# A recurrent attention kernel followed by a two-layer network: transposing DMAs, two more issuing queues and a new order

## The chip, the cores and the metric

The kernel runs on one core of a Trainium2 chip. The metric is device time in microseconds of one execution; lower is better. The core has five engines with a queue of instructions each: TensorE (PE), VectorE (DVE), ScalarE (ACT), GpSimd (POOL) and SyncE (SP). DMAs are issued from the queues of SP, ACT or POOL and run on 16 shared DMA engines.

## The reference

First a recurrence over 768 steps, for 4 batches and 8 heads of 48 channels:

```
state = zeros(B, H, D, D)
for t in range(S):
    cur = outer(u * k[t], v[t])
    y[t] = r[t] @ (state + cur)
    state = w[t][:, None] * state + outer(k[t], v[t])
```

Then, with y of all heads laid side by side (3072 rows of 384 columns), a hidden layer and an output layer:

```
h = x @ w_in                                  # 384 -> 1024
e = exp(h - max(h)); sm = e / sum(e)
solu = h * sm
ln = (solu - mean(solu)) / sqrt(var(solu) + 1e-6) * g_ln
out = ln @ w_out                              # 1024 -> 384
```

## The kernel before, in words

The rows are cut into 24 units of 128 steps: unit i is chunk i // 4 of batch i % 4. Each unit goes through a chain of stages, and each stage is a small function that issues the instructions of one unit:

- Loads: w, k, r, v of the unit (`LW`, `LK`, `LR`, `LV`; 192 KB each, in runs of 48 floats), into rings of 7 buffers (`NIO`).
- Attention: `lw` takes the log of w on ACT, `cum` sums it along the steps by two matmuls, `ex` takes exponentials, `kp` scales k and r with them on DVE (one tile `kp` of 128 x 2 x 8 x 64, bf16). `krk` and `krr` turn the scaled k and r by four TensorE transposes each into a PSUM tile `kr_ps`, and `kr` copies it to SBUF (tile `kr`, 128 x 8 x 128) on ACT or DVE. `M` multiplies them to scores, `m` copies the scores to SBUF (with the mask on DVE, or on ACT and then `sel` masks on POOL). `p`, `q`, `dg`, `dv` work out the term with u on POOL and DVE, `vb` casts v. `Y` forms y in PSUM, `y` copies it. `S`, `et`, `st` carry the state to the next chunk of the same batch.
- Network: `X` turns y by three TensorE transposes into `x_ps`, `xT` copies that to SBUF, `H` is the hidden layer (24 matmuls), `e`, `he`, `hq` its exponential, product and square, `Oa` and `Ob` the two halves of the output layer with the sums for the normalisation, `sq`, `qm`, `lv` the scale, `o` the scaled output and `out` the store.
- Once: loads of u, g and the two weight matrices (`LU`, `LG`, `LI`, `LO`), constants, casts and centring of the weights (`wi`, `gs`, `gc`, `gw`, `mn`, `mc`, `ce`), u spread over the partitions by a matmul (`us`, `uc`), and `hot`, matmuls on a zero tile.

The order is written out by hand in the string `ORDER`: one word a stage and unit, as `kr4.d`. The letter behind the dot chooses the engine or queue (a ACT, d DVE, p POOL, s SP) or, for TensorE stages, the PSUM slot. The class `InOrder` makes every engine's instructions follow in this order, so an instruction that waits holds back all that stand behind it on its engine. In the kernel before, loads stand on SP and a few on ACT, and all stores on SP. DMAs of SP and ACT share eight semaphores in turn, and a DMA waits before its issue until the one eight places earlier in the order has landed. Scores and state matmuls both read results of `kp`; the first read of a turned k and r is `M`, that of a turned y is `H`. Two functions, `turned_kr` and `turned_x` (`KD`, `XD`), stand in the table of stages and are not used:

```
sp.dma_start_transpose(out=kr_s[i % NKP], in_=kp_t[i % NKP].rearrange("t j h d -> t (j h d)"))
sp.dma_start_transpose(out=xT_t[i % NWK], in_=y_t[i % NWK])
```

The helper at line 89 records nearly all instructions, so rows of the profile are told apart by the names of tiles.

Of the kernel before, what the change touches and what calls it, by code (L numbers as in the profile page):

```python
# [8 lines left out]
F32 = mybir.dt.float32  # L9
# [12 lines left out]
LW0.a LK0.s LU0.a LR0.s LW1.a LW2.s hot4.s3 LG0.s LK1.s lw0 LV0.a cum0.b0 LR1.s us0.s0 ex0 hot2.s3 uc0 lw1 LV1.s  # L22
p0 kp0 LW3.a LK2.a LR2.s krk0.s3 q0 krr0 cum1.b1 kr0.a hot2.s2 LV2.s LK3.a M0.b0 LR3.s p1 gs0.s1 ex1 m0.d
hot3.s3 LI1.s lw2 q1 dg0 cum2.b0 lw3 hot2.s3 kp1 vb0.p LI0.a S0.s2 dv0 vb1.a dg1 hot1.s3 ex2 Y0.is0 et0 LV3.a
cum3.b1 LI2.s p2 kp2 krk1.s3 gc0 LO0.s ex3 st0 LW4.s krk2.s1 q2 krr1 LO1.s krr2 kp3 kr1.a hot3.s2 dv1 LK4.s
kr2.d y0.a p3 M1.b0 LK5.a S1.s2 dg2 krk3.s3 vb2.a m1.d krr3 et1 wi0.a S2.s0 wi1.p M2.b1 st1 X0.s1 kr3.a m2.d
Y1.is2 LR4.s wi2.p et2 y1.a M3.b0 xT0.d LV4.a X1.s3 q3 m3.d H0.b1 dv2 gw1.a dg3 gw2.d e0 Y2.is2 LW5.s xT1.d
gw3.p st2 H1.b0 y2.a he0 lw4 gw0.a X2.s1 LR5.s e1 gw7.d cum4.b1 gw4.d hot2.s3 gw6.d gw5.d ex4 he1 vb3.p mn0.s3
LW6.s LV5.a dv3 xT2.a LK6.s kp4 S3.s0 mc0 Y3.is2 LR6.s lw5 ce6.d krk4.s1 ce3.d hq0.a cum5.b0 ce4.d krr4 ce2.d
H2.b1 ce7.d ex5 LW7.s ce1.d ce5.d ce0.d y3.a LK7.s p4 kp5 et3 Oa0.s3 lw6 e2 LR7.s kr4.d p5 krk5.s2 cum6.b0 st3  # L30
hq1.a Ob0 vb4.p he2 LW8.s q4 krr5 ex6 S4.s1 LK8.s kr5.d sq0 M4.b1 lw7 Oa1.s0 kp6 et4 m4.a LR8.s X3.s2 qm0 st4
vb5.p M5.b0 xT3.a cum7.b1 dg4 sel4 lv0 krk6.s1 LV6.s Ob1 m5.d ex7 LW9.s dv4 lw8 S5.s2 kp7 o0.a krr6 LK9.s p6
cum8.b0 sq1 et5 Y4.ns3 kr6.d ex8 H3.b1 q5 LV7.s y4.d hq2.a kp8 q6 LR9.s krk7.s1 e3 X4.s3 st5 LW10.s vb6.p M6.b0
krr7 xT4.d Oa2.s2 dg5 m6.a LK10.s qm1 kr7.d dv5 krk8.s3 lv1 Ob2 he3 out0 sel6 o1.a lw9 M7.b0 out1 dg6 S6.s1 sq2
m7.a LV8.s hq3.d krr8 cum9.b1 LR10.s Y5.ns0 vb7.p qm2 kr8.d lv2 H4.b0 p7 LW11.s et6 y5.d ex9 st6 p8 lw10 kp9
LV9.s X5.s3 S7.s0 e4 Oa3.s1 q7 o2.d vb8.a he4 out2 cum10.b1 dv6 xT5.a krk9.s2 et7 LK11.s ex10 Y6.ns3 q8 krr9 st7
LV10.s H5.b0 hq4.a kp10 sel7 LR11.s kr9.a y6.d M8.b1 dg7 LW12.s S8.s0 lw11 m8.d Ob3 dv7 et8 e5 LV11.s vb9.p
krk10.s3 st8 X6.s2 LK12.s p9 M9.b1 he5 xT6.a Y7.ns0 sq3 m9.a krr10 LR12.s S9.s2 dg8 cum11.b0 et9 LW13.s y7.d
H6.b1 lw12 dv8 ex11 kr10.d LK13.s p10 qm3 lv3 kp11 Oa4.s0 LR13.s e6 q9 st9 X7.s3 cum12.b0 LW14.s xT7.a Ob4 he6
p11 ex12 LV12.s krk11.s2 sel9 sq4 Y8.ns3 o3.a kp12 H7.b1 hq5.a out3 vb10.p qm4 y8.d q10 LK14.s lv4 dg9 M10.b0 e7  # L40
Oa5.s1 LR14.s m10.d vb11.p q11 o4.a krr11 LW15.s X8.s3 lw13 dg10 Ob5 p12 xT8.a out4 he7 kr11.a S10.s0 dv9 S11.s3
LV13.s dg11 sq5 hq6.a Y9.ns2 vb12.p qm5 cum13.b0 y9.d dv10 LK15.s H8.b1 et10 ex13 st10 LR15.s et11 lw14 kp13
Oa6.s2 LW16.s e8 hq7.d krk12.s0 lw15 M11.b0 p13 st11 LK16.s Ob6 lv5 he8 o5.a q12 krr12 m11.a Y10.ns3 out5 kr12.d
krk13.s1 cum14.b1 LR16.s y10.d sq6 krr13 sel11 ex14 cum15.b0 LW17.s kr13.d Oa7.s0 ex15 qm6 LV14.s kp14 p14
Y11.ns3 lw16 X9.s1 Ob7 kp15 lv6 dv11 LK17.s vb13.a xT9.d p15 o6.a M12.b1 y11.d M13.b0 m12.a X10.s1 out6 m13.d
krk14.s2 q13 S12.s3 LR17.s hq8.a krr14 H9.b1 dg12 LV15.s vb14.p xT10.d sq7 q14 et12 qm7 st12 LW18.s lv7 krk15.s1
dg13 e9 X11.s3 sel12 H10.b0 o7.d kr14.a out7 he9 dv12 LK18.s Y12.ns0 xT11.a p16 krr15 LR18.s Oa8.s2 e10 y12.d
kr15.d q15 LV16.s cum16.b1 he10 S13.s0 ex16 dv13 Ob8 LV17.s et13 kp16 q16 X12.s3 LW19.s Y13.ns1 sq8 xT12.a st13
M14.b0 vb15.p M15.b1 LK19.s m14.a y13.d krk16.s3 S14.s0 hq9.d krr16 LR19.s m15.a S15.s1 p17 qm8 kr16.d H11.b0
LW20.s et14 dg14 lv8 sel14 st14 et15 LK20.s dg15 H12.b1 e11 vb16.p o8.d sel15 st15 out8 lw17 Oa9.s3 he11 LV18.s  # L50
e12 vb17.p dv14 S16.s0 LV19.s hq10.a he12 Ob9 dv15 LR20.s et16 cum17.b0 st16 q17 Y14.ns2 LV20.s ex17 X13.s1
y14.d M16.b1 sq9 Oa10.s0 lw18 kp17 LW21.s m16.a Y15.ns2 qm9 xT13.d LK21.s cum18.b0 hq11.d lv9 krk17.s1 lw19
H13.b1 LR21.s o9.d p18 vb18.a dg16 ex18 LV21.s y15.d dv16 krr17 e13 Ob10 kp18 LW22.s sel16 X14.s3 hq12.a kr17.d
S17.s2 LK22.s cum19.b0 q18 he13 Oa11.s1 xT14.a LR22.s ex19 p19 X15.s3 lw20 M17.b1 out9 xT15.d Ob11 sq10 kp19
vb20.p m17.a LW23.s q19 Y16.ns3 qm10 dg17 et17 vb19.a cum20.b0 p20 LV22.s y16.d lv10 H14.b1 dg18 sq11 ex20 sel17
LK23.s st17 lw21 o10.d LR23.s Oa12.s3 e14 kp20 dv17 krk18.s2 Ob12 out10 hq13.a p21 qm11 he14 krk19.s0 LV23.s
lv11 krr18 q20 cum21.b0 sq12 o11.d krr19 ex21 H15.b1 p22 qm12 kr18.d out11 lv12 kr19.d vb21.p Oa13.s1 dv18 kp21
e15 X16.s2 o12.d Y17.ns0 xT16.a M18.b0 hq14.a y17.d out12 krk20.s3 Ob13 he15 lw22 X17.s0 m18.a krk21.s2 xT17.d
krr20 cum22.b1 dg19 krr21 sq13 sel18 ex22 qm13 S18.s0 dg20 H16.b0 kr20.d hq15.a q21 kr21.d lv13 kp22 Oa14.s3
dv19 e16 dv20 M19.b1 et18 Y18.ns2 he16 m19.a Ob14 lw23 sel19 y18.d M20.b1 sq14 M21.b0 o13.d Oa15.s2 m21.a st18  # L60
out13 m20.d krk22.s1 X18.s0 cum23.b0 xT18.a krr22 Ob15 ex23 hq16.d vb22.p dg21 kr22.a Y19.ns0 q22 kp23 H17.b1
vb23.a dv21 qm14 sq15 y19.d lv14 Y20.ns1 e17 p23 o14.d H18.b0 dg22 out14 sel21 qm15 y20.d lv15 krk23.s0 he17 e18
Oa16.s3 dv22 krr23 o15.a he18 q23 Ob16 kr23.a out15 X19.s1 M22.b1 xT19.d M23.b0 hq17.d X20.s2 S19.s0 xT20.a
hq18.d Oa17.s1 m22.a dg23 Y21.ns2 et19 m23.a sel22 st19 H19.b1 sq16 sel23 qm16 y21.d lv16 Oa18.s0 e19 dv23
X21.s2 Ob17 he19 H20.b0 sq17 o16.d xT21.d out16 Y22.ns3 qm17 e20 Y23.ns2 y22.d Ob18 y23.d hq19.a he20 H21.b1
lv17 o17.d X22.s3 Oa19.s2 e21 out17 xT22.d hq20.d X23.s1 sq18 H22.b0 he21 xT23.d Ob19 qm18 hq21.d e22 H23.b1
sq19 lv18 qm19 he22 Oa20.s3 e23 o18.d hq22.d Oa21.s1 out18 lv19 he23 Ob20 o19.d Ob21 sq20 hq23.d out19 Oa22.s0
sq21 qm20 qm21 lv20 Oa23.s2 lv21 o20.d o21.d out20 Ob22 out21 Ob23 sq22 qm22 lv22 sq23 qm23 o22.d lv23 out22
o23.a out23
# [27 lines left out]
def kernel(  # L97
# [14 lines left out]
    C = 128  # L112
# [20 lines left out]
    def bank(shape, dtype, slot, name):  # L133
# [15 lines left out]
    dve.memset(warm, 0.0)  # L149
    uti_neg = consts.tile([C, C], BF16)  # L150
    pool.memset(uti_neg, -1.0)
    pool.affine_select(out=uti_neg, in_=uti_neg, compare_op=ALU.is_ge, fill=0.0, base=0,
                       pattern=[[1, C]], channel_multiplier=-1)
    uts = consts.tile([C, C], BF16)
    pool.memset(uts, 1.0)
    pool.affine_select(out=uts, in_=uts, compare_op=ALU.is_gt, fill=0.0, base=0,
                       pattern=[[1, C]], channel_multiplier=-1)
    ident_f = consts.tile([C, C], F32)
    pool.memset(ident_f, 0.0)
    pool.affine_select(out=ident_f, in_=ident_f, compare_op=ALU.not_equal, fill=1.0, base=0,  # L160
                       pattern=[[-1, C]], channel_multiplier=1)
    ident = consts.tile([C, C], BF16)
    pool.tensor_copy(out=ident, in_=ident_f)

    halves = consts.tile([C, C], BF16)
    pool.memset(halves, 0.0)
    pool.memset(halves[0:2, :], 1.0)
    pool.affine_select(out=halves[0:2, :], in_=halves[0:2, :], compare_op=ALU.is_ge, fill=0.0, base=0,
                       pattern=[[1, C]], channel_multiplier=-64)
    pool.affine_select(out=halves[0:2, :], in_=halves[0:2, :], compare_op=ALU.is_gt, fill=0.0, base=64,  # L170
                       pattern=[[-1, C]], channel_multiplier=64)
    off_blocks = consts.tile([C, HP, 2], BF16)
    pool.memset(off_blocks, 0.0)
    pool.memset(off_blocks[0:2], -30000.0)
    pool.affine_select(out=off_blocks[0:2], in_=off_blocks[0:2], compare_op=ALU.not_equal, fill=0.0, base=0,
                       pattern=[[0, HP], [-1, 2]], channel_multiplier=1)

    one_col = consts.tile([C, 2], BF16)
    dve.memset(one_col, 1.0)
    inv_col = consts.tile([C, 1], BF16)  # L180
    dve.memset(inv_col, 1.0 / RDF)
    ones_row = consts.tile([1, C], F32)
    dve.memset(ones_row, 1.0)

    lw_t = ring("lw", NLW, [C, H, 64], BF16)
    kp_t = ring("kp", NKP, [C, 2, H, 64], BF16)
    for j in range(max(NLW, NKP)):
        if j < NLW:
            dve.memset(lw_t[j][:, :, D:], 0.0)
# [366 lines left out]
```

The softmax here doesn't subtract the row's maximum and nothing guards it: scores larger than these inputs give would overflow.

## Time and profile before

| | |
|---|---|
| runs, median (lowest to highest) | 151.66 us (151.42 to 153.4) |
| profiled execution, its own time | 153.27 us |
| its span, first to last instruction | 151.6 us |
| mean granted TensorE clock | 0.994 |
| busy: PE, weight loads, DVE, ACT, POOL | 137.2, 106.6, 127.9, 117.9, 94.9 us |
| DMA | 27.08 MB, mean 179 GB/s |

The busy times are unions over the span; the rows of groups give the mean of one instruction, and neighbours on an engine overlap at their ends, so the sum over rows is larger than the busy time. A row names the engine, the operation, the tile written and those read, the count, the busy time and mean, and the idle time of the engine just before. "PEld" is TensorE's loading of weights, "SPq" and "ACTq" the issuing of DMAs by SP and ACT.

### The profile page before, as it was taken

The numbers are of one execution on the slowest core, as the hardware profiler recorded it, in microseconds if no ns is written. First come the engines' busy times: TensorE is split into PE (matmuls) and PEld (weight loads), VectorE is DVE, ScalarE is ACT, GpSimd is POOL, SyncE is SP. The second block draws the span as 40 slices with busy tenths as digits, with TensorE's granted clock in tenths as the row PEclk, the third lists the DMA queues.
The fourth block names the chain that finished last, engine by engine and source line by source line (L and its number), as shares of the span: only waits on it lengthen the run. The fifth ranks groups of instructions, "written<-read, shape, count | busy, mean of one in ns | idle before, by whom it ended". The sixth has DMA issues, their size and how long they took to land.

```text
span 151.6 us, 5258 instructions
## 1 busy us (share of the span) xinstructions
PE 137.2 (91%) x2156; PEld 106.6 (70%) x2158; DVE 127.9 (84%) x235; ACT 117.9 (78%) x238; POOL 94.9 (63%) x127
## 2 busy tenths in 40 slices
PE   4799787879999997999988999999999999999980
PEld 1145566467788776888777797878887888889650
DVE  5209797999999996999976999999998998688940
ACT  3465766599999997999798688999898997484442
POOL 7484993531879859993849999299847682500000
PEclk9999999999999999999999999999999999999997
DMA  5999999999983999989699999898950111011142
GB/s 110 259 257 334 405 335 255 178 210 188 224 179 121 229 217 193 215 176 241 142 243 208 230 175 232 162 230 193 248 164 6 52 56 52 4 52 56 52 160 104
DMA packets 104825, 27.08 MB, mean 179 GB/s; under 512 B 100313, under 2 KB 104418, under 8 KB 104802
## 3 DMA queue, kind: packets, MB, share of 16 engines
q1 hardware_dynamic: 94256, 24.26, 69.6%
q10 hardware_dynamic: 10546, 2.49, 7.3%
q8 instruction: 17, 0.28, 0.7%
q14 instruction: 6, 0.05, 0.1%
HBM read 22.03 MB, written 4.72 MB: 176 GB/s over the span
## 4 chain that ended last, share of the span: by engine, by line
PE 54%; DMA 12%; SPq 10%; DVE 8%; ACT 6%; POOL 4%; issue 4%; ACTq 0%; POOLq 0%
PE o_ps L89 22%; PE h_ps L89 13%; SPq L89 10%; DMA w_in<-in_w_dram 6%; PE kr_ps L89 4%; PE y_ps L89 4%; DMA kr_in<-in_r_dram 4%; PE s_ps L89 3%; PE cum_ps L89 3%; PE m_ps L89 3%; DMA v_in<-in_v_dram 3%; PE x_ps L89 2%; DVE he L89 1%; POOL m L89 1%; DVE w L89 1%
## 5 line engine op out<-in xcount | busy, mean ns | idle before, releaser
L89 PE MATMUL o_ps<-w,he 128*128 128x385 bf16 x192 | 45.7, 325 | 0.1
L89 PE MATMUL h_ps<-xT,win_sb 128*128 128x128 bf16 x576 | 35.9, 219 | 0.3 <-DVE xT L89 0.3
L89 PEld LDWEIGHTS <-win_sb 128*128 128x128 bf16 x576 | 33.0, 98 | 0.9 <-issue 0.4
L89 PE MATMUL o_ps<-inv_col,e 128*128 128x1 bf16 x192 | 31.7, 165 | 0.0
L89 DVE TENSOR_TENSOR he<-h_ps,e 128x1024 bf16<-128x1024 f32 x24 | 29.1, 1216 | 2.7 <-ACT e L89 2.5
L89 PE MATMUL o_ps<-one_col,hq 128*128 128x1 bf16 x192 | 31.3, 163 | 0.0
L89 ACT ACTIVATE e<-h_ps 128x1024 bf16<-128x1024 f32 x24 | 24.5, 1020 | 4.7 <-PE h_ps L89 4.6
L89 DVE TENSOR_TENSOR kp<-cum_ps,kr_in 128x768 bf16<-128x768 f32 x24 | 22.7, 948 | 5.9 <-ACT cum_ps L89 5.6
L89 PEld LDWEIGHTS <-hq 128*128 128x128 bf16 x192 | 18.5, 96 | 12.8
L89 POOL TENSOR_TENSOR p<-kr_in 128x384 bf16<-128x384 f32 x24 | 24.4, 1018 | 3.7 <-DMA kr_in<-in_r_dram 3.6
L89 POOL TENSOR_TENSOR dv<-vb,dg 128x384 bf16<-128x384 bf16 x24 | 19.8, 830 | 9.6 <-DVE dg L89 7.4
L89 POOL TENSOR_SCALAR_AFFINE_SELECT m<-m 128x1024 bf16<-128x1024 bf16 x15 | 16.8, 1120 | 13.4 <-ACT sq L89 5.8
L89 POOL TENSOR_TENSOR q<-p,u_bc 128x384 bf16<-128x384 bf16 x24 | 21.8, 911 | 1.9 <-ACT u_bc L89 1.7
L89 PEld LDWEIGHTS <-kp 128*128 128x128 bf16 x272 | 17.4, 98 | 6.0 <-DVE kp L89 2.1
L89 ACT ACTIVATE cum_ps<-cum_ps 128x768 f32<-128x768 f32 x24 | 19.2, 802 | 3.0 <-PE cum_ps L89 2.9
L89 PE MATMUL kr_ps<-ident,kp 128*128 128x128 bf16 x192 | 18.0, 222 | 2.3 <-ACT gr L89 0.8
L89 PEld LDWEIGHTS <-he 128*128 128x128 bf16 x192 | 18.4, 96 | 0.9
L89 PEld LDWEIGHTS <-e 128*128 128x128 bf16 x192 | 18.4, 96 | 0.5 <-issue 0.2
L89 ACT ACTIVATE lw<-w_in 128x384 bf16<-128x384 f32 x24 | 12.4, 523 | 4.1 <-DMA w_in<-in_w_dram 4.1
L89 ACT CAST m<-m_ps 128x1024 bf16<-128x1024 f32 x15 | 15.0, 1013 | 0.7 <-PE m_ps L89 0.6
L89 DVE TENSOR_TENSOR m<-m_ps,keep 128x1024 bf16<-128x1024 f32 x9 | 10.9, 1215 | 4.2 <-PE m_ps L89 4.2
L89 ACT ACTIVATE hq<-he 128x1024 bf16<-128x1024 bf16 x13 | 13.7, 1057 | 0.0
(82 smaller groups left out, 262.5 us busy)
## 6 DMA issues: line engine op xcount, KB each, us to landing
kr_in<-in_r_dram SPq DMA_DIRECT2D x24, 192.0 KB, 4.3
out_dram<-o SPq DMA_DIRECT2D x24, 192.0 KB, 3.2
kr_in<-in_k_dram SPq DMA_DIRECT2D x21, 192.0 KB, 3.5
w_in<-in_w_dram SPq DMA_DIRECT2D x21, 192.0 KB, 4.2
v_in<-in_v_dram SPq DMA_DIRECT2D x20, 192.0 KB, 4.1
wout_f<-in_moe_w_out_dram SPq DMA_DIRECT2D x2, 768.0 KB, 7.7
win_f<-in_moe_w_in_dram SPq DMA_DIRECT2D x2, 512.0 KB, 5.1
v_in<-in_v_dram ACTq DMA_DIRECT2D x4, 192.0 KB, 4.2
```

Of the source, the lines that this page charges most:

```text
L89: made = make(*args, **kwargs)
```

## The change

- `LV` is issued by ACT for 21 of 24 units (4 before); two of the first r loads, and the first w and k, by ACT too. g is loaded by POOL's queue, and the constants, written ahead of everything before, become a stage `pc` behind that load. u is loaded by SP.
- 16 of the 24 stores are issued by POOL (`out4.p` and the like), 8 by SP.
- In 14 units (7, 8, 12 to 23) by the words of the order, `X` and `xT` give way to `XD`, a transposing DMA from SP; in 14 units (9 to 11, 13 to 23) `krk`, `krr` and `kr` give way to `KD`.
- u is rounded to bf16 (`ur` on DVE) and spread by a bf16 matmul.
- All stages stand in a new order, with other choices of engine: `kr` copies that remain 2 on ACT and 8 on DVE (8 and 16 before), `xT` 4 and 6 (12 and 12), `o` 13 and 11 (8 and 16), `hq` 10 and 14 (13 and 11), `vb` 5 on ACT and 19 on POOL (7 and 17), `ce` 5 on DVE and 3 on POOL (8 and 0), `wi` 3 on ACT (1, and 2 on POOL); `hot` 32 matmuls (19).

The order, cut to its beginning, a stretch with the first of the new DMAs, and its end:

```diff
-LW0.a LK0.s LU0.a LR0.s LW1.a LW2.s hot4.s3 LG0.s LK1.s lw0 LV0.a cum0.b0 LR1.s us0.s0 ex0 hot2.s3 uc0 lw1 LV1.s
...
-sq21 qm20 qm21 lv20 Oa23.s2 lv21 o20.d o21.d out20 Ob22 out21 Ob23 sq22 qm22 lv22 sq23 qm23 o22.d lv23 out22
-o23.a out23
+LG0.p pc0 LR0.a LU0.s LW0.a LW1.s hot3.s3 LK0.a LW2.s LW3.s gs0.s0 hot5.s3 LK1.s lw0 LR1.a ur0 cum0.b0 hot2.s3
...
+lv2 dg8 X6.s0 q9 Oa3.s3 e5 KD9 st8 xT6.d dv7 S9.s2 hq4.a he5 cum12.b1 KD10 p10 Y7.ns0 et9 ex12 Ob3 st9 dv8 y7.d
+LV11.a LR13.s H6.b0 kp12 lw13 p11 LW14.s hq5.a KD11 dg9 Y8.ns2 p12 o2.d sq3 krk12.s0 e6 M9.b1 y8.d dv9 Oa4.s1
+XD7 qm3 m9.a he6 q10 S10.s2 lv3 LK14.s krr12 cum13.b1 out1.p et10 kr12.d LR14.s Ob4 ex13 sel9 dg10 LW15.s Oa5.s0
...
+Oa23.s1 sq21 out20 qm21 lv21 Ob22 o21.d Ob23 out21 sq22 qm22 lv22 sq23 qm23 o22.d lv23 o23.a out22.p out23.p
```

The code (the body of `constants` holds the memsets and selects that stood in line before, in the same sequence on POOL and on DVE):

```diff
-    ones_row = consts.tile([1, C], F32)
-    dve.memset(ones_row, 1.0)
+    ones_row = consts.tile([1, C], BF16)
...
+    def constants(i, x):
+        dve.memset(warm, 0.0)
+        pool.memset(uti_neg, -1.0)
...
+    u_b = consts.tile([1, DM], BF16)
...
-    queue = {"s": sp, "a": act}
+    queue = {"s": sp, "a": act, "p": pool}
...
+    def round_u(i, x):
+        dve.tensor_copy(out=u_b, in_=u_row)
+
     def spread_u(i, x):
         ps["u"] = bank([C, DM], F32, x, "u_ps")
-        pe.matmul(ps["u"], lhsT=ones_row, rhs=u_row, start=True, stop=True)
+        pe.matmul(ps["u"], lhsT=ones_row, rhs=u_b, start=True, stop=True)
...
     def store(i, x):
         c, b = units[i]
-        sp.dma_start(out=out[b * S + c * C:b * S + (c + 1) * C, :], in_=o_t[i % NWK])
+        queue[x or "s"].dma_start(out=out[b * S + c * C:b * S + (c + 1) * C, :], in_=o_t[i % NWK])
...
     stages = dict(
+        pc=constants,
...
+        ur=round_u, us=spread_u, uc=copy_u, gs=turn_g, gc=copy_g, wi=cast_w_in, gw=gain, mn=column_mean, mc=copy_mean,
```

## The prediction

> **What bounds the kernel now.** I read the chain that ended last first, because it says which engine the end hangs on, then the table by stretches, then the waits, then the queues. In the chain by time, the first and the last row of TensorE's own stretch and three pieces between:
>
> ```profile
> 33.73 0.99 PE o_ps L89 x12
> ...
> 57.28 1.35 PE h_ps L89 x24
> ...
> 96.20 1.34 PE h_ps L89 x24
> ...
> 126.19 0.27 PE x_ps L89 x3
> ...
> 140.38 5.98 PE o_ps L89 x84
> ```
>
> From 33.73 us (the first half output, Oa0) to 146.36 us nearly every piece is a TensorE stage. Ahead of it the chain is loads and their issue. The busy time by stretches (us; PE, PEld, DVE, ACT, POOL, then clock, DMA share, GB/s):
>
> ```profile
> 0.00:33.73 33.73, 26.24 (x266) 15.45 (x268) 22.97 (x57) 20.57 (x37) 21.78 (x41) 1.00 1.08 262
> 33.73:60.00 26.27, 25.72 (x435) 20.77 (x435) 24.86 (x41) 24.25 (x50) 18.84 (x23) 1.00 0.91 190
> 60.00:85.00 25.00, 23.17 (x396) 18.98 (x396) 22.46 (x37) 22.39 (x45) 19.41 (x24) 1.00 0.96 207
> 85.00:110.00 25.00, 24.93 (x432) 20.72 (x430) 24.77 (x44) 22.59 (x47) 21.49 (x26) 1.00 1.00 208
> 110.00:140.40 30.40, 30.40 (x539) 26.02 (x538) 27.09 (x48) 23.60 (x46) 13.41 (x15) 1.00 0.17 54
> ```
>
> TensorE is full, VectorE and ScalarE are some 5 to 10% behind it, and the DMA engines are occupied until about 110 us. So work taken off TensorE pays only if VectorE and ScalarE lose work too, and if nothing new on the DMA side comes late. What the removed work costs, from the groups of instructions (count, busy us, mean ns, idle before):
>
> ```profile
> L89 PE MATMUL kr_ps<-ident,kp 128*128 128x128 bf16 x192 | 18.0, 222 | 2.3 <-ACT gr L89 0.8 <-DVE kp L89 0.7 <-ACT o L89 0.7
> ...
> L89 DVE COPY kr<-kr_ps 128x1024 bf16<-128x1024 bf16 x16 | 10.7, 679 | 0.0
> ...
> L89 ACT COPY kr<-kr_ps 128x1024 bf16<-128x1024 bf16 x8 | 8.1, 1015 | 1.2 <-PE kr_ps L89 1.2
> ...
> L89 PE MATMUL u_ps<-u_row,ones_row 1*128 1x384 f32 x2 | 1.6, 923 | 0.0
> ```
>
> What the loads cost their queues, from the tiles of w and v (least, median and longest ns of an issue), and then one line of the waits (us in total, times, longest):
>
> ```profile
> L89 SPq DMA_DIRECT2D w_in<-in_w_dram x21: 379/842/4202, 1.9 to 104.5; - x21
> ...
> L89 SPq DMA_DIRECT2D v_in<-in_v_dram x20: 379/957/1732, 5.5 to 108.3; - x20
> L89 ACTq DMA_DIRECT2D v_in<-in_v_dram x4: 374/374/379, 4.3 to 29.9; - x4
> ...
> DMA to landing us min/median/max: 3.2/4.1/8.0
> ```
>
> ```profile
> ACT xT L89 <- DMA w_in<-in_w_dram: 1.9, 1, 1.9
> ```
>
> The reader sees two things for later: a load holds SyncE's queue 0.84 to 0.96 us and lands 4.1 us after its issue; and ScalarE, which itself issues only 12 loads, once stands 1.9 us in front of an unrelated copy because its next load had to wait for an earlier DMA.
>
> **What the Trainium skill says.** "VectorE: DVE Perf Modes", The three transpose paths: 1309 ns for a 128x128 bf16 transpose by DMA, 390 by TensorE. The trace has no transposing DMA; TensorE's own shows 222 ns each and four of them 0.22 to 0.25 us in the chain, because they overlap. "DMA: Bandwidth & Descriptors", Issuing engines are not separate DMA queues: DMAs from all issuers run on the same 16 engines, and another issuer saves only the sequencer's time. This fits the landing times, 4.1 us for v on SyncE's queue and 4.2 on ScalarE's. Same page, Specifications: about 1 us to the first byte for a DMA that GpSimd issues, 0.6 from the others; the trace has none from GpSimd. "SBUF — State Buffer", SBUF: two separate sides: VectorE's two-port modes can hold up GpSimd's writing of descriptors; no run here shows it.
>
> **The change, part by part.** TensorE stages are taken from the chain: hidden layer 1.34, half an output 0.83, four transposes 0.225, x turned 0.18, state 0.47, scores 0.33, y 0.38, cumulation 0.33.
>
> 1. Turned k and r. By the new order 14 units (9 to 11, 13 to 23) lose 2 x 0.225 on TensorE: 6.3 us. Their copies leave VectorE (8 x 0.68 = 5.4) and ScalarE (6 x 1.015 = 6.1).
> 2. Turned y. 14 units (7, 8, 12 to 23) lose 0.18: 2.5 us of TensorE; the copies, 6 x 0.35 on VectorE and 8 x 0.48 on ScalarE.
> 3. Order. Summed by the stages above, TensorE has 19.0 us ahead of Oa0 in the old order, 26.7 in the new (7.0 instead of 4.2 of it warming matmuls). Behind Oa0 it has 108.0 before and 94.2 after: 13.8 less, of which 8.8 are steps 1 and 2 and 5.0 moved ahead of Oa0, where TensorE was idle 7.5 us. Behind Oa0, with the mean durations of the rows, VectorE falls from 116.3 to 101.5 and ScalarE from 110.7 to 93.9. These two overlap their own neighbours (the rows' sum is 10% over the busy time), so both stay under TensorE.
> 4. Start. The second w_out load now stands behind 20 loads instead of 17. 0.59 MB at the 262 GB/s of the first stretch is 2.2 us. ScalarE's work ahead of Oa0 also rises, from 22.3 to 30.7. I put Oa0 at 37.0, with bounds 35.0 and 39.0.
> 5. u in bf16: the two f32 passes of 923 ns become one of about 0.35. It lies in the stretch bound by loads; I count nothing. If it were on the path it would gain 1.2.
> 6. v by ScalarE. 17 more loads there at 0.37 us, 6.3 us of its sequencer; they issue while the previous activation runs, and ScalarE has slack after losing 9 us of copies. The risk is the wait of the kind quoted above: a DMA's semaphore is shared with the eighth DMA before it in program order, and these are now partly transposes on SyncE. Behind such a wait stand exp, log and all copies of ScalarE.
> 7. Stores by GpSimd. 16 stores leave SyncE's queue, where waits for o held it (25 us on VectorE's o in the waits of SP, mostly at the end). On GpSimd I price a store at 1.0 us, an estimate after the skill's first-byte figure; bounds 0.1 and 2.0. From Oa0 to Oa12 GpSimd then has 59.8 us beside TensorE's 54.1. Part of the excess 5.7 is hidden in the waits it has now (9.6 us ahead of dv); I take 1.2 us of late masks and bonus terms.
> 8. The transposing DMAs. For k and r 256 KB in one DMA, for y 96 KB. From the load of 192 KB (4.1 to landing): low 2.8 (the shortest landing of a k or r load), high 8 blocks x 1.309 = 10.5 us. I take 5.0 for k and r and 3.0 for y, because bytes and piece counts are close to a load's. Between the issue of the turned pair and its scores the new order gives TensorE this much other work, units 9 to 11 and 13 to 23: 4.0, 7.0, 4.8, 5.7, 9.1, 4.7, 11.3, 9.6, 4.1, 4.5, 4.9, 5.0, 4.5, 4.9. At 5.0 the shortfalls add to 3.6; for y at 3.0, where units 20 to 23 have 2.7, 1.6, 2.5 and 3.0, to 2.2. A stall also lengthens the time for the next transpose, so I count 0.6 of 5.8: 3.5 us. Behind the waiting scores stands everything on TensorE.
>
> The idle time of TensorE that is there now from Oa0 on is 112.6 - 108.0 = 4.6; about 1.3 of it is waits at turned k and r, so 3.3 stays. The last stores go by GpSimd: the tail, 151.6 - 146.4 = 5.2, becomes 5.8.
>
> Sum: 37.0 + 94.2 + 3.3 + 3.5 + 1.2 + 5.8 = 145.0 us of span. The profiled execution took 153.27 with a span of 151.6; the median of the runs is 151.66, 1.6 below that execution, so that span and median happen to agree and 145.0 stands for the median.
>
> **The rivals.**
> - All is hidden (stores cheap, transposes inside their slack): 145.0 - 3.5 - 1.2 gives 140.3. For it: the order has at least 4.0 us behind each turned pair. Against: the loads' 4.1 us to landing is a median, the longest 8.0.
> - GpSimd becomes the bound up to unit 12: at 2.0 us a store it has about 9 us more than above in that stretch, of which 6 come through: 151. For it: GpSimd is at 21.5 of 25 us from 85 to 110. Against: half of its idle time is waiting for others.
> - The transposes hold SyncE's queue, and slower is the result. From Oa8 to Oa16 the new order gives it 19 plain DMAs at 0.84, 16 us, in 34 us of TensorE's work and waits; the other 18 are for 6 turned pairs and 7 turned y, as many bytes as 8.6 pairs. So above 2.1 us of queue a pair, the queue is late, each landing is later, the loads behind are too, and ScalarE stands at v loads that share a semaphore. With a landing of 7.5 us the shortfalls add to 28.4, at 0.6 that is 17 in place of 2.2: 145 + 15 = 160. It decides from a landing of about 6.2 us (break-even) or 6.7 (slower by 2%). For it: 8 blocks at the skill's price; 9 of the 14 slacks are 5.0 or less. Against: by bytes a pair is only 1.33 of a load, 1.1 us of queue.
> - That the change does not do what it says can be excluded: the new order carries 28 transposing DMAs.
>
> **How the numbers follow.** Forecast case 0.38 (145, own range 141 to 148), all hidden 0.12, GpSimd 0.15 (149 to 154), SyncE's queue 0.35 (155 to 170). Range 139 to 163: it takes in the first two wholly, GpSimd's, and the larger part of the last. Faster by over 2% (about what a measurement of this kernel can tell from no change) 0.50, within 0.15, slower 0.35.
>
> **What would show it.** Right: first o_ps matmul at 35 to 39 us; transposes landing in about 5 us and holding SyncE's queue under 2 us; TensorE's busy time near 130 (137.2 - 8.8 + 2.9 of warming - 1.2); waits of TensorE for transposing DMAs of 2 to 5 us in all. Wrong: waits at m_ps or h_ps for DMA over 10 us, ScalarE waiting for DMA in the middle of the run, GpSimd over 90% busy from 40 to 100 us, or the first o_ps after 40 us.

## The result, and the profile after

The changed kernel takes 165.14 us (median of 4 runs, 163.46 to 167.42) where the kernel before took 151.74 beside it: ratio 1.0822, 95% interval 1.0692 to 1.0953. It is slower by 8%; the forecast was 145.0. Ratios here leave out runs more than 1.5% above the fastest of their kernel, so they can differ from the quotient of the two medians. The profiled execution of the changed kernel took 163.46 us, with a span of 161.7 and a mean TensorE clock of 0.973. All numbers of the changed kernel below are of that execution, if nothing else is said.

First the chain that ended last, by engine, then six of its pieces in order of time (start, length, what):

```profile
DMA 26%; DVE 15%; issue 14%; SPq 13%; PE 12%; ACT 9%; POOL 8%; ACTq 1%; POOLq 0%; DVEq 0%
```

```profile
20.90 8.86 DMA kr_in<-in_r_dram
...
81.33 6.72 DMA kr<-kp
...
99.74 5.49 DMA xT<-y
105.23 0.05 issue
105.28 2.74 PE h_ps L85 x24
...
117.37 3.44 DMA kr_in<-in_r_dram
...
125.87 4.80 DMA kr_in<-in_r_dram
```

The chain is no longer TensorE's (12% of the span; 54% in the kernel before). It runs through loads and through both kinds of transposing DMA, and one hidden layer, released by a transpose, takes 2.74 us instead of 1.34. The table by stretches from the first half output, at 42.8 us, to the last, at 156.1 (columns as before: PE, PEld, DVE, ACT, POOL, clock, DMA share, GB/s):

```profile
42.80:60.00 17.20, 16.74 (x265) 12.72 (x263) 17.13 (x27) 15.41 (x33) 13.60 (x17) 1.00 1.01 182
60.00:85.00 25.00, 23.65 (x412) 19.32 (x409) 22.77 (x38) 20.55 (x42) 22.51 (x28) 1.00 1.09 221
85.00:110.00 25.00, 20.02 (x312) 16.10 (x310) 17.24 (x29) 16.66 (x38) 17.17 (x22) 0.93 1.19 181
110.00:135.00 25.00, 22.70 (x384) 18.18 (x380) 21.31 (x33) 18.05 (x38) 17.21 (x22) 1.00 1.20 207
135.00:156.10 21.10, 17.60 (x292) 14.10 (x290) 16.91 (x26) 11.78 (x27) 6.17 (x9) 1.00 0.42 107
```

From 60 us on no engine is full, but the DMA engines' share stands at 1.09 to 1.20, and it stays there until 135 us, where in the kernel before it had fallen to 0.17 after 110. Against the forecast's span the excess is 161.7 - 145.0 = 16.7 us, in four terms:

| | forecast | measured | |
|---|---|---|---|
| first half output | 37.0 | 42.8 | +5.8 |
| TensorE busy from there to the last (sum of the table) | 94.2 | 100.7 | +6.5 |
| TensorE idle in it | 3.3 + 3.5 + 1.2 = 8.0 | 113.3 - 100.7 = 12.6 | +4.6 |
| tail | 5.8 | 161.7 - 156.1 = 5.6 | -0.2 |

Of the 6.5 us more of busy time, 4.0 stand in the kernel without the transposes too (98.2, below), and 1.7 are a stretch at half clock behind 105 us (last section).

The removed work, from the groups of instructions, and the new DMAs, from the tiles (least, median and longest ns for which one holds SyncE's queue; below each, the time from issue to landing):

```profile
L85 PE MATMUL kr_ps<-ident,kp 128*128 128x128 bf16 x80 | 7.1, 219 | 0.5 <-DVE st L85 0.4
...
L85 PE MATMUL u_ps<-u_b,ones_row 1*128 1x384 bf16 x1 | 0.3, 331 | 0.0
```

```profile
L85 SPq DMA_TRANSPOSE kr<-kp x14: 1232/1828/4092, 54.6 to 132.7; - x14
...
DMA to landing us min/median/max: 3.2/5.0/6.7
```

```profile
L85 SPq DMA_TRANSPOSE xT<-y x14: 1186/1426/2827, 62.5 to 143.9; - x14
...
DMA to landing us min/median/max: 2.3/4.3/5.5
```

The waits that answer to the forecast's list (total, times, longest):

```profile
POOL p L85 <- DMA kr_in<-in_r_dram: 11.8, 5, 5.6
...
PE h_ps L85 <- DMA xT<-y: 4.3, 3, 1.8
...
PE m_ps L85 <- DMA kr<-kp: 2.9, 3, 1.6
...
ACT et L85 <- DMA kr_in<-in_r_dram: 1.9, 1, 1.9
```

TensorE waits 7.2 us for transposing DMAs themselves. The largest wait for a DMA is GpSimd's, for plain r loads. Those stand in SyncE's queue behind the transposes, and a stretch of that queue shows how (start, time held, what):

```profile
92.94 1.15 SPq L85 DMA_DIRECT2D w_in<-in_w_dram  x1
94.17 1.55 SPq L85 DMA_TRANSPOSE xT<-y  x1
95.82 0.53 SPq L85 DMA_DIRECT2D kr_in<-in_k_dram  x1
96.44 2.58 SPq L85 DMA_TRANSPOSE kr<-kp  x1
99.07 0.57 SPq L85 DMA_DIRECT2D kr_in<-in_r_dram  x1
99.74 4.13 SPq L85 DMA_TRANSPOSE xT<-y  x2
103.93 0.57 SPq L85 DMA_DIRECT2D w_in<-in_w_dram  x1
```

Each row starts where the one before it ends, within 0.1 us. From 81.3 to 126.5 us the queue has no longer gap than that: it is full for 45 us. A full queue is no loss by itself: in the kernel before, from 60 to 100 us, it has gaps of 0.5 us in all, with loads that hold it 0.88 us each on average. What is new is what the loads now share it with. The six turned pairs from 81.3 to 119.8 hold it 4.09, 2.87, 2.58, 2.79, 2.73 and 1.80 us, 2.8 on average; the median over the whole run, 1.83, hides this.

### The profile page after: what moved, and what is told of

Read it like the earlier page. It is cut to its first block, busy times and chain, and to the rows that moved or that the text cites. A ratio compares the mean times of both kernels' runs of the same rounds, so it can differ in the third digit from the quotient of the medians.

```text
span 161.7 us, 5030 instructions
## 1 busy us (share of the span) xinstructions
PE 133.7 (83%) x2017; PEld 101.5 (63%) x2017; DVE 127.5 (79%) x217; ACT 112.0 (69%) x226; POOL 107.9 (67%) x147
## 4 chain that ended last, share of the span: by engine, by line
DMA 26%; DVE 15%; issue 14%; SPq 13%; PE 12%; ACT 9%; POOL 8%; ACTq 1%; POOLq 0%; DVEq 0%
SPq L85 13%; DMA kr_in<-in_r_dram 11%; DMA xT<-y 6%; DMA kr<-kp 4%; DVE kp L85 4%; PE o_ps L85 3%; DMA w_in<-in_w_dram 3%; ACT e L85 3%; DVE he L85 3%; DMA out_dram<-o 3%; PE h_ps L85 3%; POOL dv L85 2%; PE s_ps L85 1%; POOL out_dram L85 1%; POOL m L85 1%
## 5 line engine op out<-in xcount | busy, mean ns | idle before, releaser
L85 PE MATMUL o_ps<-w,he 128*128 128x385 bf16 x192 | 45.9, 325 | 0.0
L85 PE MATMUL h_ps<-xT,win_sb 128*128 128x128 bf16 x576 | 37.1, 223 | 5.8 <-DMA xT<-y 4.3
L85 PEld LDWEIGHTS <-win_sb 128*128 128x128 bf16 x576 | 34.2, 100 | 7.4 <-DMA xT<-y 3.0
L85 POOL TENSOR_TENSOR p<-kr_in 128x384 bf16<-128x384 f32 x24 | 23.9, 999 | 14.0 <-DMA kr_in<-in_r_dram 11.8
L85 ACT ACTIVATE e<-h_ps 128x1024 bf16<-128x1024 f32 x24 | 24.6, 1023 | 10.8 <-PE h_ps L85 10.5
L85 POOL DMA_DIRECT2D out_dram<-o x16 | 9.1, 572 | 14.2 <-ACT o L85 8.5
L85 PEld LDWEIGHTS <-kr 64*128 64x128 bf16 (+1 forms) x272 | 10.5, 96 | 6.9 <-DMA kr<-kp 3.6
L85 DVE TENSOR_TENSOR hq<-he 128x1024 bf16<-128x1024 bf16 x14 | 14.0, 997 | 0.1
```

The source lines that it names most:

```text
L85: made = make(*args, **kwargs)
```

## The experiments

All ratios are to the kernel before, run on the same chip at the same time; its median was 152.5 to 154.2 us in these groups, so kernels of different groups are compared by ratio. "First output" is the start of the first o_ps matmul in the profiled execution, a single one for each kernel. x1, x5 and z3 have the words of the changed kernel up to there, and start at 46.8, 45.9 and 47.6 us where it starts at 42.8: in the new order differences of a few us between two kernels' first outputs tell nothing by themselves. Kernels with the old words up to there spread less, from 33.7 to 35.0.

### What the transposes cost: constants in place of turned tiles

z1 is the changed kernel, but scores, the old-state part of y and the hidden layer of the turned units read constant tiles; the DMAs are still issued. z2 leaves them out too. Both set the constant tiles by two more memsets of GpSimd at the start. x1 and x5 put the transposes back on TensorE.

```diff
 # z1; z2 also without the words KD.. and XD..
-        xT = xT_t[i % NWK]
+        xT = xT_fix if i in XD_UNITS else xT_t[i % NWK]
 # x1, in the order, for each of the 14 + 14 (the copy right behind; x5 spreads them)
-KD13
+krk13.s2 krr13 kr13.d
-XD12
+X12.s0 xT12.a
```

> The changed kernel in which nothing reads what the 28 transposing DMAs write: the scores and the old state's part of y of those 14 units read a constant tile, and so does the hidden layer of the 14 units with turned y. The DMAs are issued as before. So TensorE has no wait for a landing, while SyncE's queue and the DMA engines carry the same load. Theory B (waits for landing are the loss; 7.2 us of TensorE's idle time, and the clock that falls after them): 152-156. Theory A (the queue and the loads behind): 162-165. Theory C (the order and its start): 157-160.

> As z1, with the 28 transposing DMAs left out altogether: turned tiles for nothing, the best that the new order could do with v on ScalarE and stores on GpSimd. Against z1 it prices what the transposes cost on SyncE's queue and the DMA engines. Theory A: 8 or more under z1, 148-153. Theory B: at most 2 under z1. Theory C: even so not under 154, slower than the kernel before, for the start stays at 43 to 48 us.

Measured: z1 163.47 us, ratio 1.0431 [1.0307, 1.0555]; z2 153.2 us, ratio 0.9881 [0.9835, 0.9927]. The stretches of z1, then of z2, from their first half output (46.9 and 46.3 us) on:

```profile
60.00:85.00 25.00, 23.13 (x402) 18.88 (x401) 24.63 (x40) 20.73 (x45) 23.62 (x30) 1.00 1.06 197
85.00:110.00 25.00, 24.00 (x388) 19.03 (x386) 21.93 (x35) 20.33 (x44) 19.83 (x25) 0.93 1.22 203
110.00:135.00 25.00, 21.37 (x356) 16.94 (x354) 19.46 (x29) 16.74 (x33) 15.12 (x19) 1.00 1.07 199
...
sum 111.40, PE 102.01 PEld 80.82 DVE 97.88 ACT 82.81 POOL 76.40; mean PE 20.40 PEld 16.16 DVE 19.58 ACT 16.56 POOL 15.28
```

```profile
60.00:85.00 25.00, 25.00 (x443) 20.62 (x444) 24.11 (x42) 22.09 (x46) 23.81 (x30) 1.00 0.75 170
85.00:110.00 25.00, 24.70 (x421) 19.86 (x419) 23.29 (x39) 21.16 (x47) 22.73 (x28) 1.00 0.94 202
110.00:135.00 25.00, 24.38 (x430) 19.99 (x428) 22.92 (x36) 19.79 (x39) 19.86 (x26) 1.00 0.32 89
...
sum 99.60, PE 98.21 PEld 78.60 DVE 93.07 ACT 81.61 POOL 77.28; mean PE 19.64 PEld 15.72 DVE 18.61 ACT 16.32 POOL 15.46
```

By their medians z1 lies in the range named for the queue and z2 at the upper end of its own. Two things follow. With the transposes for nothing TensorE has 1.4 us of idle time in 99.6, so the reduced work does run as forecast, and the new order still wins only 1.2%, because its first output comes at 46.3 us. And transposes for which nothing waits cost 1.0431 - 0.9881 = 5.5% of the time, 8 us (by the two intervals 1.3% to each side): they lift the DMA share from 0.75 to 1.06 and from 0.32 to 1.07, and in the profile of z1 GpSimd waits 8.5 us for r loads between its first and last output, in z2 not at all. The waits for the turned tiles themselves are the rest, 1.0822 - 1.0431 = 3.9%, 6 us (1.8% to each side). This split is rough: z1's ratio rests on two of its four runs, 159.27 and 161.57 us, the others took 165.37 (the one with the profile) and 166.4; with all four the waits would be worth less and the transposes more.

> The changed kernel with all 28 transposing DMAs taken back: krk, krr, kr and X, xT on TensorE and its copies at about the same places of the order; v on ScalarE, stores on GpSimd and the rest of the new order stay. Theory A (the transposes hold SyncE's queue 1.8 and 1.4 us each, and the loads behind them, placed only some 40 words ahead of their use, come late): the waits of GpSimd's p for r loads fall from 11.8 to under 4 us, and the time falls to 155-158 although TensorE has 8.8 us more work. Theory B (TensorE waits for the landing of the turned tiles themselves, 7.2 us in the trace): 157-159, with p's waits still over 8 us. Theory C (the loss is in the start and in the order, whatever turns the tiles): 165-172, because the 8.8 us come back on TensorE and nothing else changes.

> The changed kernel without transposing DMAs, as x1, but with the TensorE transposes and their copies spread over the room between their producer and their reader (1 to 1.3 us of other TensorE work between transposes and copy, 2.4 us or more behind the copy), because in x1 the copies stood right behind the transposes and TensorE waited for them. Theory C (the new order, with its queues, is slow by itself): still 168-173. Theory A (the transposes and their hold of SyncE's queue are the loss, and x1 hid that by its tight places): 155-160.

Measured: x1 173.87 us, ratio 1.1379 [1.1291, 1.1466]; x5 169.36 us, 1.1012 [1.0944, 1.108]. GpSimd's wait for r loads went, as it should, but taking the DMAs out of this order and TensorE's transposes in was slower still. The order has no room for the copies: in x1 GpSimd waits 20.7 us for scores copied by ScalarE, and VectorE's busy time in x5 is 135 us. x1 lies above all its ranges, and x5 in the one named for a loss by the new order itself, but z2 shows that order at 0.9881 where turned tiles cost nothing. These two do not say what the DMAs cost; z2 does.

### The parts alone, in the order before

b1 takes v of the same units by ScalarE, b2 the same 16 stores by GpSimd, b3 the 28 transposes, b6 those of y alone, b5 all three. The words concerned change and nothing else.

```diff
-LV8.s      # b1
+LV8.a
-out8       # b2
+out8.p
-krk13.s1 krr13 kr13.d X12.s3 xT12.a    # b3, each DMA right behind kp and y
+KD13 XD12
```

> The kernel before with one part of the change alone: v of the same 21 units as in the changed kernel is issued by ScalarE, at the places of the old order. If ScalarE's standing at v loads that wait for a shared semaphore is a main part of the loss: 157-160. If the new order is what loses (theory C): 150-154, nothing beyond 2%.

> The kernel before with the same 16 stores as in the changed kernel issued by GpSimd, the rest and the order as before. A store held GpSimd 0.58 us in the changed kernel, 9.1 us in all. If stores on GpSimd that wait for o hold up its masks and bonus terms (rival of the prediction): 156-160. Theory C: 150-154.

> The kernel before with the transposing DMAs alone: k and r of the same 14 units and y of the same 14 units are turned by SyncE, issued directly behind kp and behind y in the old order; everything else as before, stores and v on SyncE too. TensorE loses 8.8 us. Theory C (transposes are no loss, as taking them out of the changed kernel made it 9 us slower): 143-152. Theory A (SyncE's queue, now with all stores and most v loads beside 28 transposes, is late): 158-175. Theory B (landing times of 5.0 and 4.3 us against TensorE's other work): 153-158.

> The old order with the three parts together: v on ScalarE, 16 stores on GpSimd, 28 transposing DMAs on SyncE. Theory A (SyncE's queue is what the transposes overload; b3 with stores and v on it gave 174.7): the queue is relieved of some 33 issues, 22 us, so 160-166, near the changed kernel. Theory D (each part adds its own loss: 2.7, 4.1 and 21 us): 178-182. Theory C (the new order is at fault): 155-158.

> The old order with only y of the 14 units turned by DMA: 14 issues of 1.2 to 1.4 us on SyncE, 18 us of its queue, where turning k and r as well took 42. Theory A: loss in proportion to the queue time, 157-163. Theory B (waits for landing, y's slack is 2.2 to 10 us and a landing 3.1): 152-156.

| | us | ratio | first output |
|---|---|---|---|
| b1, v by ScalarE | 156.23 | 1.0187 [1.0119, 1.0255] | 38.3 |
| b2, stores by GpSimd | 158.05 | 1.0269 [1.0157, 1.0382] | 33.8 |
| b3, 28 transposes | 174.71 | 1.1412 [1.1306, 1.1518] | 34.8 |
| b6, y of 14 units | 157.55 | 1.0223 [1.0139, 1.0307] | 35.0 |
| b5, all three | 175.77 | 1.1445 [1.1358, 1.1533] | 38.4 |

Every part loses by itself (b1, b2 and b6 not surely by as much as 2%), and the turned k and r lose most: b3 less b6 is 12%. In b3 the DMAs land sooner than in the changed kernel (median 3.8 us for k and r, 3.1 for y), and TensorE waits 9.0 us for them. What is late besides is again what stands behind them:

```profile
POOL vb L84 <- DMA v_in<-in_v_dram: 14.8, 5, 4.1
...
ACT lw L84 <- DMA w_in<-in_w_dram: 10.6, 4, 4.3
```

In b1 the loss is all at the start: behind its first output TensorE idles 1.0 us in all. The wait that does it, and the stretches around it:

```profile
ACT cum_ps L87 <- DMA win_f<-in_moe_w_in_dram: 4.7, 1, 4.7
```

```profile
12.00:15.00 3.00, 0.33 (x2) 0.10 (x1) 1.22 (x2) 0.00 (x0) 0.83 (x1) 0.95 1.03 393
15.00:21.00 6.00, 4.24 (x29) 2.39 (x29) 2.84 (x4) 3.04 (x8) 2.70 (x3) 0.50 1.16 334
```

An exponential that needs no weights stands 4.7 us for w_in: ahead of it in ScalarE's queue is a k load, issued only at 14.85 us, and the trace names a w_in load as what ended the wait, which fits two DMAs that share a semaphore. TensorE then idles, and its clock is 0.50 for the next 6 us. b5 repeats it: a wait of 4.8 us for w_in, and the first output at 38.4.

In b2 a store takes GpSimd only 0.58 us, as in the changed kernel, but it is issued by an engine that must first wait for o:

```profile
POOL out_dram L88 <- DVE o L88: 20.0, 6, 7.0
```

b5 speaks against the number of issues on SyncE's queue as the sole cause: it takes 33 of them away from b3, and the queue theory named 160 to 166 us for it, but it is no faster. It does lie below the sum of the parts, 1.187, so the relief may be hidden by what v and the stores cost on their new engines. In its trace the queue is nearly as full as in b3 (from 60 to 135 us gaps of 1.1 us in all, in b3 0.7); there are fewer plain loads in it, but one holds it 0.98 us on average, where b3 has 0.73. So the time that an issue takes may follow the load on the DMA engines; no run separates the queue from the engines, for instance with the transposes issued by ScalarE.

### Undoing a part in the new order

```diff
-LV8.a  out8.p  ce4.p      # x3; z3; x4 (three centrings)
+LV8.s  out8    ce4.d
 # x2: loads of units 7 to 23 about 100 words ahead of their use instead of 23 to 60
```

> The changed kernel with the loads of units 7 to 23 moved ahead in the order, to about 100 words before their first use (23 to 60 now); the transposes stay where they are. Theory A: the loads no longer stand behind the transposes that wait, p's waits for r loads nearly vanish, 155-159. Theory B: the turned tiles land when they did or later (more loads ahead of them in the queue), 163-168. Theory C: no change, 164-166.

> The changed kernel with v of units 4 to 23 issued by SyncE again, at the same places. Theory A: SyncE's queue gets 17 more issues of 0.7 us, 12 us, in front of loads that are late already: 167-172. If instead ScalarE's standing at v loads that wait for a shared semaphore (3.2, 2.0 and 1.9 us seen in its waits) is a main loss: 159-162. Theory B: 164-167.

> The changed kernel with all 8 centring additions of w_out on VectorE (3 of them on GpSimd in the changed one). In the changed kernel's trace the centring took 5.5 us from the mean to the last addition, against 3.0 in the kernel before, with both engines at it. Theory C: the first output matmul moves from 42.8 to about 40 us and the time falls by 2 to 3 us, 162-163. Theories A and B: the first output comes earlier but the later waits take it back, 164-166.

> The changed kernel with all stores on SyncE. In the old order the stores on GpSimd cost 2.7% (b2). If that holds here: 160-162. Theory A: SyncE's queue gets 16 issues of 0.5 us more and stands at stores that wait for o, in front of transposes and loads: 167-172.

Measured, the changed kernel being at 1.0822 [1.0692, 1.0953]: x2 166.36 us, 1.0788 [1.0678, 1.0898]; x3 167.9, 1.0944 [1.0838, 1.105]; x4 163.13, 1.0658 [1.0568, 1.0747]; z3 168.9, 1.0968 [1.0891, 1.1045]. x2 moved the wait without shortening anything: GpSimd's wait for r fell from 11.8 to 2.1 us, and TensorE's for the turned tiles rose from 7.2 to 10.1. Whatever comes first in the queue, something else comes late at its reader. x3 and z3 put 17 loads or 16 stores back into SyncE's queue. Both times lie in the range named for a queue without room (167 to 172 us), but their intervals overlap that of the changed kernel, so that they are slower is not shown; what they show is that the losses of b1 and b2 are not won back there. x4, less by 2 us, is not told apart from the changed kernel either.

### Why the first output is late

> The changed kernel with another start: both w_out loads ahead of the third w_in load, v of units 4 to 6 on SyncE, scaling and centring of w_out on VectorE (one scaling on GpSimd), the centring additions in one piece. Theory C: the first output matmul comes at 38 to 41 us instead of 43 to 48, and the time falls by most of that, 158-161. Theories A and B: the earlier start is taken back by the waits behind it, 163-166.

> This is the kernel without transposing DMAs, whose scores, old-state part of y and hidden layer read constant tiles in the turned units, with seven instructions ahead of the first half output moved from VectorE to ScalarE: y of units 1 and 2, four copies of turned y, one square of he. Start to start they take VectorE 2.6 us. If VectorE's own queue sets the start (to the end of the last centring it has 29.7 us of work by 41.0 in the changed kernel, 22.9 by 33.7 in the one before, and idles 11 us in both), the first o_ps comes 2 to 3 us earlier, near 43.5 instead of 46.3, and the time is near 150.5, ratio 0.97. If the loads or ScalarE's waits set it, nothing moves or it gets later (ScalarE has 3.9 us more): 153 to 155.

> The changed kernel with the same seven moved. VectorE theory: 1 to 3 us less than the changed kernel, 162 to 164, first o_ps near 41 to 44. Other theory: 165 to 168.

x8 puts the w_out loads ahead of the third w_in load, v of units 4 to 6 on SyncE, and scaling (but for one part) and centring on VectorE, most of the centring in one piece; s1 (on z2) and s2 (on the changed kernel) move seven instructions ahead of the first output from VectorE to ScalarE:

```diff
-y1.d y2.d xT0.d xT1.d xT2.d hq1.d xT3.d
+y1.a y2.a xT0.a xT1.a xT2.a hq1.a xT3.a
```

Measured: x8 166.07 us, 1.0779 [1.0698, 1.086], first output 47.5; s1 152.62, 0.995 [0.9909, 0.999], first output 45.8 (z2: 46.3); s2 163.36, 1.0582 [1.0493, 1.0671], first output 44.8. None is ahead of the 42.8 to 47.6 us that the same head shows without these edits. In x8 the chain stands at the third w_in load, now behind w_out in the queue: it landed at 27.6 us, 9.4 after its issue. Whether VectorE sets the start is not settled. Against it: s1 is not faster than z2, its VectorE idled longer, 3.5 us for an exponential of ScalarE and 2.0 for another, and the centring ended only 0.4 us earlier. For it: s2's time lies in the range named for VectorE, and its ratio 2.4% under the changed kernel's, with intervals that just don't meet.

The profile of z2 shows the delay coming from ScalarE around 17 to 25 us: 1.4 us for w_in at a DMA's semaphore and 2.4 for the v load that was therefore issued late, at 17.0, and landed 6.7 us later. Its chain there (start, length, what):

```profile
11.89 5.12 DMA win_f<-in_moe_w_in_dram
...
17.02 6.71 DMA v_in<-in_v_dram
```

The chains of x1, z1, z3 and s2 have the same two pieces within 1 us. The changed kernel's own chain has another of the kind: ScalarE stands 1.9 us in front of `et` until the r load issued at 20.90 has landed, 8.86 us later. b1 shows that v by ScalarE alone costs 4.6 us of start in the old order (38.3 against 33.7). TensorE's clock goes with it: ahead of the first output it is at half rate for 3.4 us in the changed kernel and for 6.8 in z2, and not at all in the kernel before; how much of the start that costs was not measured. Taking v back within the first 20 us of the new order was not tried, and how the 9 to 14 us there divide between these waits, the slow centring, the clock and the larger work ahead of it stays open.

### A few turned tiles at the end

b4 turns only k and r of units 20 to 23 and y of 17 to 23, with stores 11 to 19 by GpSimd, in the old order; in b7 the stores stay on SyncE. There the loads are through: the DMA share had fallen to 0.17 in that stretch.

```diff
-krk20.s3 krr20 kr20.d X17.s0 xT17.d    # b7: units 20 to 23, y of 17 to 23
+KD20 XD17
```

> The kernel before with transposing DMAs only where the loads are done: k and r of units 20 to 23, y of units 17 to 23, and the stores of units 11 to 19 issued by GpSimd so that they don't stand before the transposes on SyncE. TensorE loses 4 x 0.45 + 7 x 0.18 = 3.1 us in the stretch in which it has no gap. Theory C: 147-150, faster than both. Theory A: the same, for there are no loads to hold up. Theory B: 151-154, landing times of some 3 to 5 us stall TensorE.

> The old order with transposing DMAs where the loads are done (k and r of units 20 to 23, y of units 17 to 23), all stores on SyncE as before; in b4 nine of them were on GpSimd and ate the gain, if the loss of b2 is theirs. Then 148.5-151. If the late transposes themselves bring nothing because their landing stalls TensorE: 151-154, as b4.

Measured: b4 154.67 us, 1.0002 [0.9943, 1.0062]; b7 152.53 us, 0.9931 [0.9892, 0.997]. b7 is the only complete kernel here that is faster than the one before, by 0.7%, less than the 2% that the prediction takes for what a measurement can tell from no change. Its 152.53 us lie in the range named for transposes that bring nothing: of the 3.1 us of work taken from TensorE about 1 shows in the time.

## Why the prediction was wrong, step by step

The likeliest case fell with steps 4 and 8; the range ended 2 us below the result. What happened comes nearest to the rival of SyncE's queue (forecast 160, chance 0.35), by another route than it named, and with a late start on top.

1. and 2. Turned k, r and y: right as to TensorE. The row of k and r fell from 192 to 80 matmuls, and in z2 the whole stretch from first to last half output takes 99.6 us, where these steps with step 3 and the leftover idle time gave 94.2 + 3.3 = 97.5. By terms, TensorE is busy 98.2 in it at full clock and idle 1.4: the sum of stages was 4 us short, the leftover idle 2 too high. Half of that could be seen beforehand: the profile before has TensorE busy for 110.2 us between its first and last half output, where the prediction sums 108.0.
3. Order: right as to the work behind the first output, in z2. That VectorE and ScalarE stay under TensorE held there too (93.1 and 81.6 beside 98.2). It left out that those engines have more to do ahead of it.
4. Start: failed. 37.0 with bounds 35 to 39, measured 42.8, and 44.8 to 48.1 in the other kernels with this head or one near it. The step summed the bytes ahead of w_out and ScalarE's busy time. TensorE's work in that stretch was a term without a price: step 3 sums 19.0 us ahead of Oa0, but the prediction's own table shows 26.24 busy there. With the 7.7 us that the new order adds it makes 33.9 (32.8 measured), so a start at 37.0 left TensorE 3 us of idle time where it had 7.5. The step did not look for the waits in ScalarE's own queue of step 6, nor at the centring: that took from 35.5 to 41.1 us, 3 of 8 on GpSimd beside VectorE and with other work between, where the 8 on VectorE had taken 2.5 us. In z2, without anything from transposes, this step is 46.3 - 37.0 = 9.3 us and turns the forecast of "all hidden", 140.3, into a span of 151.6.
5. u in bf16: 331 ns against 0.35 us forecast, and nothing on the path.
6. v by ScalarE: the named risk was the right one, but its place was the start and not the middle, and it was costed at nothing: 4.6 us of start in b1, where the ratio is 1.0187.
7. Stores: the price was too high, 0.58 us against 1.0, and the cost too low. Not the issue counts, but the wait for o ahead of it with masks and products behind: 2.7% in b2, 4 us, against 1.2.
8. Transposing DMAs: landing of k and r was right (5.0 median), of y too low (4.3 against 3.0); TensorE's waits for them, 7.2 us, are twice the 3.5. What failed is the argument against the rival, "by bytes a pair is only 1.33 of a load, 1.1 us of queue". A pair holds the queue 1.83 us in the median, and 2.8 where the queue is full, above the 2.1 from which the rival decides. The likeliest case had no term at all for the plain loads behind the transposes, and by the rough split above that is the larger part: 8 us between z1 and z2, where nothing waits for a transpose. The rival's own route, a landing of 6.2 us and later scores, did not show: the damage came through the loads behind, by way of the queue and the DMA engines together.

The Trainium skill, "DMA: Bandwidth & Descriptors", Issuing engines are not separate DMA queues, had told half of it: other issuers save only the sequencer's time on the same 16 engines. b5 agrees, where v and stores from other queues beside the transposes gained nothing over b3 (175.77 and 174.71 us). What z1 and z2 add is that a transpose takes its share of these engines as well (0.75 to 1.06). The price of 1309 ns for one 128x128 block (quoted in the prediction) does not add up over 8 blocks, as the bound of 10.5 us had it: the longest landing is 6.7.

Of the signs named, landings near 5 us came out right, and TensorE's busy time of 133.7 nearly (about 130 forecast; 132.8 in z2); the first o_ps after 40 us was a sign of failure, and so were ScalarE's waits for DMAs in the middle (3.2 us ahead of sq, for a transpose, and 2.0 ahead of lw, for a store). TensorE's waits for transposes, 7.2 us, lie between the sign for right and that for wrong. Over 90% of GpSimd from 40 to 100 us was not seen.

## What to carry to other kernels

Price a DMA that replaces compute by how long it holds its queue and the 16 engines while loads run, and by what stands behind it there, not only by its landing beside its reader; where the loads are over (b7) the same transposes at least cost nothing. In front of a stretch bound by one engine, walk through every engine's queue up to the first instruction of that stretch: add up the bounding engine's own work there from its measured busy time. A start that comes 6 to 9 us late eats the whole gain of such a stretch. When DMAs move to a computing engine's queue, the price is the waits that they bring into it, for a shared semaphore or for the data of a store.

## What the runs showed of the hardware

**A gap of 2 us can halve TensorE's clock for 3.4 us or more.** The hidden layer at 105.28 us took twice its time after TensorE had waited 1.8 us for its input. The changed kernel in stretches of 3 us:

```profile
102.00:105.00 3.00, 1.51 (x24) 1.03 (x21) 2.52 (x3) 2.88 (x9) 2.69 (x4) 1.00 0.51 134
105.00:108.00 3.00, 2.72 (x26) 2.53 (x28) 0.66 (x3) 0.10 (x1) 0.68 (x2) 0.55 1.01 220
```

Taken in steps of 1 us, the half rate lasts 3.4 us, and so 1.7 us of work are lost. In b3 there are five such stretches behind the first output, four of 3.4 us and one of 6.8 (mean clock of the run 0.929), each after a gap of 2.1 us or more; in b1 one of 6.8. But the length of the gap does not decide alone: in the changed kernel gaps of 1.5, 1.6 and 2.0 us (ahead of 146.57, 124.79 and 137.07) had no such stretch behind them. The Trainium skill, "TensorE: Matmul & The Clock Gate", Part 1: The HAM clock gate, puts the fall to half rate after at least one idle window of about 3.4 us; here one wait of 1.8 us, after 4 us of work without a gap, was enough. This was no term of the forecast.

**VectorE stands behind GpSimd.** The square hq, two inputs from SBUF, takes VectorE 0.69 us in the median, but:

```profile
L85 DVE TENSOR_TENSOR hq<-he x14: 680/692/2858, 34.7 to 152.6; 128x1024 bf16<-128x1024 bf16 x14
```

The longest began at 134.16, and from 134.56 to 136.45 GpSimd ran these two:

```profile
134.56 1.10 POOL L85 TENSOR_SCALAR_AFFINE_SELECT m<-m 128x1024 bf16<-128x1024 bf16 x1
135.62 0.83 POOL L85 TENSOR_TENSOR dv<-vb,dg 128x384 bf16<-128x384 bf16 x1
```

0.69 plus their 1.9 us is 2.6 of the 2.86, and TensorE stood 2.0 us in front of the output layer that reads this square. It fits the Trainium skill, "SBUF — State Buffer", SBUF: two separate sides, by which such a VectorE operation and one of GpSimd exclude each other for the whole instruction. The order is not explained: the square is on record 0.4 us ahead of the first of the two, and still it was the one that waited. The centring shows the effect too: 0.35 us each on VectorE alone, in the kernel before, and 1.0 in the median beside GpSimd's. x4, which takes only GpSimd's three additions to VectorE, has 0.34 in the median again. For the square no run isolated it.
